# Drawing twelve attention halves into the first six parts of the weight stage, and loading the first unit's queries first

## The chip, the cores and the metric

The kernel runs on one core of one Trainium2 chip. The metric is device time in microseconds (us) of one execution, lower is better. A core has TensorE (PE), VectorE (DVE), ScalarE (ACT) and GpSimd (POOL), which run their own instruction streams in order, and SyncE (SP), whose queue issues nearly all loads of this kernel, in order as well.

## The reference, cut to what matters

Window attention over 8 heads, then two feed-forward blocks, all in float32. The last weight of the first block is only ever used behind `w3`, so the kernel may multiply `w3 @ w_out` ahead of the tokens.

```python
scores = q @ k.T / sqrt(64)            # 4 x 8 heads, 576 positions, head size 64
attn   = softmax(where(0 <= i - j < 64, scores, -1e9)) @ v
x      = attn laid out as [2304, 512]
x      = ((x @ w1) * (x @ w2)) @ w3 @ w_out      # 512 -> 1024 -> 1024 -> 512
h      = x @ w_in                                # 512 -> 2048
out    = (h * sigmoid(h)) @ w_out2               # 2048 -> 512
```

## The kernel before, in words

The weights come as 64-bit words and are converted on the chip. A chunk is 128 x 512 weights, 512 KB of words. `line` (40 chunks in the first stage) is the order in which they are worked. `loads_to(n)` issues the loads up to chunk n on SP's queue (L107). `steps_to(n)` advances the conversion: `stage0` is two ACT instructions (L114, L115), `stage1` two DVE instructions ("fraction", L125, and "sign", L128) and a POOL addition (L132). The two `stage1` pieces are put on a list, `parts`, and `fill` puts them out between other DVE instructions. Chunks of `w1` and `w2` also get a high part (ACT, L140) and a low part (DVE or POOL, L144).

The first stage, `phase_w` (L401), multiplies `w3 @ w_out`. It has 16 steps s of two parts each, 32 parts in all. A part first advances the conversion by about one chunk (`steps_to`, L468), then puts out attention (`halves_to`, L469), then four PE matmuls of 128 x 512 (L476, two accumulators, each shown as two instructions in the trace). In front of each s, `loads_to` asks for the chunks of two steps ahead (L462). By that order each engine and SP's queue meet: loads of chunks, conversion, attention, matmuls, part by part. Four accumulators are emptied after part 15 and 16 and again after part 31 and 32 (ACT and DVE, L483 by way of `split`, L79 and L82).

Attention is worked in groups g (one unit of 128 tokens, one pair of heads). A group takes two halves. Half 2g transposes the weights of group g-1 on PE (L308), makes the scores of group g (L261), and then masks and takes the row minimum on DVE (L275, two instructions), copies the transposed weights on ACT (L314) and takes the exponentials on ACT (L286). Half 2g+1 normalises on DVE (L294, L296, L298), multiplies group g-1 with its values on PE (L335 to L337), copies that on ACT (L338), and asks SP for the queries and keys of group g+2 (`load_qk`, L219 and L223, three loads) and the values of group g+2 (`load_v`, L229). The buffers of queries and keys are two, so `load_qk(g+2)` waits until PE has made the scores of group g; `load_v(g+2)` waits until PE has multiplied the values of group g-1. In the first block's groups (g < 17, "plain") this is all there is.

When enough halves are out, `split_x(0, c)` (L473) splits a quarter of the attention's output for the next stage. After the 32 parts `phase_a(0)` (L486) begins with half 28, which transposes group 13 and makes the scores of group 14. Phase A and all that follows are mostly matmuls.

Of the kernel before, what the change touches and what calls it, by code (L numbers as in the profile page):

```python
# [42 lines left out]
def tile_window_attention_ffn(ctx, tc, qkv, vp, mask, ident, w1, w2, w3t, w_out, w_in, w_out2, out):  # L43
# [15 lines left out]
    def f32(ap):  # L59
        return ap.bitcast(F32)  # L60
# [7 lines left out]
    def slot(name, tag, dims, dtype=F32, pool=None, bufs=1):  # L68

        t = (pool or main).tile([128, SLOTS.get(tag, 1024)], dtype, name=name, tag=tag, bufs=bufs)  # L70
        n = int(np.prod(dims))
        letters = "abcd"[: len(dims)]
        sizes = {x: d for x, d in zip(letters[1:], dims[1:])}
        return t[:, :n].rearrange(f"p ({' '.join(letters)}) -> p {' '.join(letters)}", **sizes)
# [14 lines left out]
    def accumulator(name, shape):  # L89

        turn[0] = (turn[0] + 1) % converting["banks"]
        return ps.tile(shape, F32, name=name, tag=f"ps{turn[0]}")
# [59 lines left out]
    def loads_to(n):  # L152
        while done["load"] < min(n, len(line)):
            if line[done["load"]]:
                line[done["load"]].load()
            done["load"] += 1
# [8 lines left out]
    def steps_to(n, lo=(nc.vector,), keep=0):  # L165

        while done["step"] < min(n, len(line)):
            t = done["step"]
            loads_to(t + 1)
            fill(len(parts))  # L170
            if t >= 1 and line[t - 1]:
                parts.extend(line[t - 1].stage1())
            fill(len(parts) - keep)
            if t >= 4 and line[t - 4]:
                line[t - 4].low_part(lo[t % len(lo)])
            if t >= 3 and line[t - 3]:
                line[t - 3].high_part()
            if line[t]:
                line[t].stage0()
            done["step"] += 1  # L180

    def drain():
        line.extend([None] * 4)
# [18 lines left out]
    def plain(g):  # L202


        return g < PLAIN

    def place(g):
        blk, r = divmod(g, 3 * NPAIR)
        return blk * 3 + r % 3, r // 3

    def load_qk(g):
        if g < NG and g not in loaded:
            loaded.add(g)
            qk_raw[g] = att.tile([128, 768], F32, name=f"qk{g}", tag="qk", bufs=2)
            u, c = place(g)
            if not plain(g):
                nc.sync.dma_start(out=qk_raw[g], in_=qkv[u, c, :, 0:768])
                return
            nc.sync.dma_start(out=qk_raw[g][:, 0:128], in_=qkv[u, c, :, 0:128])  # L219

            for h, hs in HEADS:
                n = slice(384 + h * 192, 576 + h * 192)
                nc.sync.dma_start(out=k_p[g % 2][hs, h * 192 : h * 192 + 192], in_=qkv[u, c, hs, n])  # L223

    def load_v(g):
        if g < NG and ("v", g) not in loaded:
            loaded.add(("v", g))
            if plain(g):
                nc.sync.dma_start(out=v_p[g % 3], in_=vp[g])  # L229
                return  # L230
            v_raw[g] = att.tile([128, 3, 64], F32, name=f"v{g}", tag="v", bufs=3)
            u, c = place(g)
            nc.sync.dma_start(out=v_raw[g].rearrange("p t d -> p (t d)"), in_=qkv[u, c, :, 768:960])
# [119 lines left out]
    def half(h):  # L353


        g, odd = divmod(h, 2)
        if not odd:
            t_ps = transposes(g - 1) if 1 <= g <= NG else None
            if g < NG:
                scores(g)  # L360
            if t_ps is not None:
                split_t(g - 1, t_ps)
            if g < NG:
                exps(g)
        else:
            if g < NG:
                normalise(g)
            if 1 <= g <= NG:
                values(g - 1)
            for x in (g + 1, g + 2):  # L370
                if x - g == (1 if plain(x - 2) else 2):
                    prep_qk(x)
            if g < NG:
                prep_v(g)

            for x in range(g + 2, g + 5):
                if g < (x - 2 if plain(x - 2) else x - 4):
                    break
                load_qk(x)
            for x in range(g + 1, g + 4):  # L380
                if g < (x - 2 if plain(x - 3) else x - 3):
                    break
                load_v(x)
# [3 lines left out]
    def halves_to(n):  # L387
        while halves[0] < min(n, LAST_HALF):
            half(halves[0])
            halves[0] += 1  # L390
# [8 lines left out]
    W_HALVES = 28  # L399

    def phase_w():  # L401
        wo = slot("wo", "p", [8, 512])
        q = slot("q", "q", [2304])
        for i in range(2):
            p_w.append(att.tile([128, 384], F32, name=f"pw{i}", tag="vhl", bufs=2)[:, 0:320])
        w3x = [q[:, i * 512 : i * 512 + 512] for i in range(4)]
        w3x += [att.tile([128, 512], F32, name=f"w3x{i}", tag=f"pt{i}", bufs=1) for i in range(3)]
        ring = [("st", 4)] * 4 + [(f"w{i}", 1) for i in range(20, 24)]
        words = [0]

        def add(key, src, out):
            tag, bufs = ring[words[0] % 8]
            words[0] += 1
            line.append(Chunk(key, src, (main, tag, bufs), out))

        def add_w3(s):
            sw, j = divmod(s, 8)
            add(None, w3t[j * 128 : (j + 1) * 128, sw * 512 : (sw + 1) * 512], w3x[s % 7])

        def add_w12(i):  # L420
            src = (w1, w2)[i // 8][(i % 4) * 128 : (i % 4 + 1) * 128, (i // 4 % 2) * 512 :][:, :512]
            line.append(Chunk(("12", i), src, (main, f"w{i}", 1)))

        ready, i12 = [], 0
        order = (0, 1, 2, 3, 8, 9, 10, 11, 4, 5, 6, 7, 12, 13, 14, 15)
        for s in range(16):
            if s < 8:
                add(None, w_out[s * 128 : (s + 1) * 128, :], wo[:, s])
            add_w3(s)
            ready.append(len(line) + 1)  # L430
            while i12 < W12_BY[s]:
                add_w12(order[i12])
                i12 += 1
        while i12 < 16:
            add_w12(order[i12])
            i12 += 1
        drain()
        ready += [W12_B + 24 + (4 if W12_B == 16 else 0)] * 2

        for t in k_p + [f32(t) for t in k_lo]:  # L440
            for h, hs in HEADS:
                nc.gpsimd.memset(t[hs, 192 - h * 192 : 384 - h * 192], 0.0)
        loads_to(2)
        load_qk(0)
        nc.sync.dma_start(out=mask_sb[:, 1], in_=mask[:, 1])
        loads_to(3)
        nc.sync.dma_start(out=id_sb, in_=ident)
        load_v(0)
        load_qk(1)
        loads_to(5)  # L450
        nc.sync.dma_start(out=mask_sb[:, 0], in_=mask[:, 0])
        load_v(1)
        loads_to(6)
        load_v(2)
        steps_to(ready[0])
        nc.sync.dma_start(out=mask_sb[:, 2], in_=mask[:, 2])
        half(0)
        halves[0] = 1
        acc, split_done = {}, set()
        for s in range(16):  # L460
            sw, j = divmod(s, 8)
            loads_to(ready[s + 2] + (3 if s > 1 else 0))  # L462
            if j == 0:
                for i in range(4):
                    acc[i] = accumulator(f"accw{sw}_{i}", [128, 512])
            for part in range(2):
                first = ready[s + 1 if s else 0]
                steps_to(first + (ready[s + 2] - first) * (part + 1) // 2, (nc.vector, nc.gpsimd), 3)  # L468
                halves_to(min(W_HALVES, 2 + W_HALVES * (2 * s + part + 1) // 32))  # L469
                for c in range(4):  # L470
                    if halves[0] >= 6 * c + 8 and (0, c) not in split_done:
                        split_done.add((0, c))
                        split_x(0, c)  # L473
                fill(3)
                for i in (0, 1) if part == 0 else (2, 3):
                    nc.tensor.matmul(  # L476
                        acc[i], lhsT=w3x[s % 7][:, i * 128 : (i + 1) * 128], rhs=wo[:, j],
                        start=(j == 0), stop=(j == 7),
                    )
                    if j == 7:  # L480
                        n = sw * 4 + i
                        wp[n] = slot(f"wp{n}", f"w{16 + n}", [2, 512], F32R)
                        split(wp[n][:, 0], wp[n][:, 1], acc[i], "act", "dve")  # L483
# [272 lines left out]
```

## Time and profile before

| | us |
|---|---|
| three runs | 884.69, 1725.24, 883.5 |
| their median | 884.69 |
| the profiled execution | 884.13 |
| its span, first to last instruction | 882.3 |
| first part's matmuls begin | 9.65 |
| sixth part's matmuls begin | 30.81 |
| half 28, the end of the 32 parts | 103.88 |

The span is what the trace shows; 1.8 us of the execution lie around it. The second of the three runs took twice the time of the others and stands for nothing in the kernel. Rows of the timeline are: start in us, duration in us, engine, line, operation, output<-input, count, and in brackets the idle time before it and what ended that.

### The profile page before, as it was taken

The numbers are of one execution on the slowest core, as the hardware profiler recorded it, in microseconds if no ns is written. First come the engines' busy times: TensorE is split into PE (matmuls) and PEld (weight loads), VectorE is DVE, ScalarE is ACT, GpSimd is POOL, SyncE is SP. The second block draws the span as 40 slices with busy tenths as digits, with TensorE's granted clock in tenths as the row PEclk, the third lists the DMA queues.
The fourth block names the chain that finished last, engine by engine and source line by source line (L and its number), as shares of the span: only waits on it lengthen the run. The fifth ranks groups of instructions, "written<-read, shape, count | busy, mean of one in ns | idle before, by whom it ended". The sixth has DMA issues, their size and how long they took to land.

```text
span 882.3 us, 13255 instructions
## 1 busy us (share of the span) xinstructions
PE 856.0 (97%) x4362; PEld 737.0 (84%) x4362; DVE 480.7 (54%) x1202; ACT 491.0 (56%) x1219; POOL 430.6 (49%) x474
## 2 busy tenths in 40 slices
PE   4998999999999999999999999999999999999997
PEld 2454689999999999999999888888888888888896
DVE  5889888878888888888365886111111111111111
ACT  5778677788787788787475775222222222222322
POOL 4558476466466466465395787222322232222222
PEclk9999999999999999999999999999999999999999
DMA  8888423333432323331477500200020001000100
GB/s 286 295 251 262 134 79 99 125 99 100 127 94 90 126 90 100 119 99 50 182 277 261 202 0 1 77 20 0 1 89 7 0 1 51 22 0 1 48 1 25
DMA packets 43205, 85.84 MB, mean 97 GB/s; under 512 B 4864, under 2 KB 22528, under 8 KB 43136
## 3 DMA queue, kind: packets, MB, share of 16 engines
q1 hardware_dynamic: 37088, 75.55, 26.4%
q10 hardware_dynamic: 6048, 9.44, 2.9%
q8 instruction: 35, 0.57, 0.3%
q14 instruction: 34, 0.28, 0.1%
HBM read 75.53 MB, written 9.44 MB: 96 GB/s over the span
## 4 chain that ended last, share of the span: by engine, by line
PE 86%; DVE 2%; POOL 1%; issue 1%; ACT 0%; DMA 0%; POOLq 0%; SPq 0%; DVEq 0%
PE h L627 23%; PE o L646 22%; PE ab L504 21%; PE x L524 11%; PE t L308 2%; PE o L343 2%; PE s L265 1%; PE s L269 1%; PE accw L476 1%; PE o L344 1%; POOL klo L244 1%; DVE cv_b L128 0%; DVE cv_z L125 0%; DVE rs L294 0%; PE s L261 0%
## 5 line engine op out<-in xcount | busy, mean ns | idle before, releaser
L82 POOL TENSOR_TENSOR g<-sg,g 128x512 fp32r<-128x512 f32 (+1 forms) x80 | 94.8, 1185 | 250.0 <-ACT g L79 237.3
L627 PE MATMUL h<-x2t,hl 128*128 128x512 f32 (+1 forms) x960 | 213.4, 371 | 0.0
L646 PE MATMUL o<-hl,g 128*128 128x512 f32 x864 | 211.2, 392 | 0.4 <-ACT g L79 0.3
L633 DVE TENSOR_TENSOR sg<-h,sg 128x512 f32<-128x512 f32 (+1 forms) x80 | 51.1, 638 | 288.5 <-ACT sg L632 288.5
L627 PEld LDWEIGHTS h<-x2t,hl 128*128 128x128 f32 x960 | 169.4, 188 | 33.8
L646 PEld LDWEIGHTS o<-hl,g 128*128 128x128 f32 x864 | 160.9, 188 | 35.9 <-ACT g L79 0.8
L632 ACT ACTIVATE sg<-h 128x512 f32<-128x512 f32 (+1 forms) x80 | 44.4, 555 | 195.4 <-PE h L627 195.4
L504 PE MATMUL ab<-xa,hl 128*128 128x384 f32 x576 | 117.1, 338 | 0.0
L504 PE MATMUL ab<-xb,hl 128*128 128x384 f32 x576 | 115.6, 335 | 0.0
L504 PEld LDWEIGHTS ab<-xb,hl 128*128 128x128 f32 x576 | 101.4, 188 | 0.0
L504 PEld LDWEIGHTS ab<-xa,hl 128*128 128x128 f32 x576 | 99.8, 188 | 0.8
L351 POOL TENSOR_TENSOR xr<-ot 128x128 f32<-128x128 f32 x55 | 33.2, 603 | 118.5 <-DVE ot L350 116.5
L132 POOL TENSOR_TENSOR cv_b<-cv_b,cv_r 128x512 int32<-128x512 int32 x48 | 73.6, 1534 | 26.8 <-DVE cv_b L128 11.2
L79 ACT CAST g<-sg 128x512 fp32r<-128x512 f32 (+1 forms) x80 | 46.3, 579 | 63.5 <-DVE sg L633 61.8
L286 ACT ACTIVATE sm<-sm,nm 128x192 f32<-128x192 f32 x144 | 64.4, 448 | 17.7 <-DVE nm L275 16.6
L244 POOL TENSOR_TENSOR klo<-qk,qkhi 64x192 fp32r<-64x192 f32 x110 | 70.1, 637 | 5.7 <-ACT qkhi L240 1.5
L524 PE MATMUL x<-p,wp 128*128 128x384 f32 x360 | 69.6, 335 | 0.0
L524 PEld LDWEIGHTS x<-p,wp 128*128 128x128 f32 x360 | 62.2, 188 | 0.1
L125 DVE TENSOR_SCALAR cv_z<-cv_b 128x512 int32<-128x512 int32 x72 | 49.4, 686 | 17.0 <-ACT cv_b L114 16.6
L114 ACT ACTIVATE cv_b<-words 128x512 f32<-128x512 f32 x72 | 48.2, 670 | 11.5 <-DMA words<-in_w_out 5.6
L128 DVE SCALAR_TENSOR_TENSOR cv_b<-words,cv_z 128x512 int32<-128x512 int32 x72 | 49.4, 686 | 3.5 <-issue 0.5
L275 DVE CUSTOM_DVE_ANT_0 sm<-s,mask_sb 128x192 f32<-128x192 f32 x144 | 45.7, 354 | 6.6 <-PE s L261 3.6
(82 smaller groups left out, 1258.9 us busy)
## 6 DMA issues: line engine op xcount, KB each, us to landing
qk<-in_qkv SPq DMA_DIRECT2D x55, 384.0 KB, 3.1
words<-in_w_out SPq DMA_DIRECT2D x24, 512.0 KB, 8.4
words<-in_w3t SPq DMA_DIRECT2D x16, 512.0 KB, 6.2
words<-in_w SPq DMA_DIRECT2D x16, 512.0 KB, 6.2
words<-in_w_in SPq DMA_DIRECT2D x16, 512.0 KB, 6.8
v<-in_qkv SPq DMA_DIRECT2D x55, 96.0 KB, 2.7
x2d<-x2s ACTq DMA_DIRECT2D x24, 192.0 KB, 1.9
out_x<-osb ACTq DMA_DIRECT2D x18, 256.0 KB, 2.1
```

The source lines that it names most:

```text
L82: (nc.vector if eng_lo == "dve" else nc.gpsimd).tensor_tensor(out=lo, in0=src, in1=f32(hi), op=ALU.subtract)
L114: nc.scalar.activation(out=f32(self.b), in_=f32(self.high), func=AF.Copy, scale=2.0**-112)
L125: nc.vector.tensor_scalar(out=self.z, in0=b, scalar1=3, scalar2=None, op0=ALU.logical_shift_left)
L128: nc.vector.scalar_tensor_tensor(out=b, in0=self.high, scalar=-0x80000000, in1=self.z, op0=ALU.bitwise_and, op1=ALU.bitwise_or)
L132: nc.gpsimd.tensor_tensor(out=x, in0=b, in1=self.r, op=ALU.add)
L244: nc.gpsimd.tensor_tensor(out=k_lo[g % 2][hs, h * 192 : h * 192 + 192], in0=t[hs, n], in1=f32(hi[hs, n]), op=ALU.subtract)
L286: nc.scalar.activation(out=x, in_=x, func=AF.Exp, scale=-1.0, bias=nm[:, h : h + 1], accum_out=rs[:, h : h + 1])
L504: nc.tensor.matmul(acc, lhsT=w[:, l, fs], rhs=x[k // 2][:, k % 2, r, :], start=(k == 0 and n == 0), stop=(k == 3 and n == 2),)
L524: nc.tensor.matmul(acc, lhsT=wp[f][:, l, o * 128 : (o + 1) * 128], rhs=p[f][:, r, :], start=(f == 0 and n == 0), stop=(f == 7 and n == 2),)
L627: nc.tensor.matmul(acc, lhsT=weights["in", f // 4, k][:, l, fs], rhs=x[:, k, r, :], start=(k == 0 and i == 0), stop=(k == 3 and i == 2),)
L633: nc.vector.tensor_tensor(out=sg, in0=acc, in1=sg, op=ALU.mult)
L646: nc.tensor.matmul(oacc[t], lhsT=g[:, l, t * 128 : (t + 1) * 128], rhs=weights["out", f][:, r, :], start=(f == 0 and i == 0), stop=(f == 1 ...
```

## The change

Two edits, both in `phase_w`. The loads of group 0's queries and keys are issued ahead of the first two chunks instead of behind them. The count of halves up to part n (n from 1 to 32) becomes 2 + min(2n, 9 + 17n // 32) instead of 2 + 28n // 32, both at most 28.

```diff
                 nc.gpsimd.memset(t[hs, 192 - h * 192 : 384 - h * 192], 0.0)
+        load_qk(0)
         loads_to(2)
-        load_qk(0)
         nc.sync.dma_start(out=mask_sb[:, 1], in_=mask[:, 1])
...
                 steps_to(first + (ready[s + 2] - first) * (part + 1) // 2, (nc.vector, nc.gpsimd), 3)
-                halves_to(min(W_HALVES, 2 + W_HALVES * (2 * s + part + 1) // 32))
+
+                n = 2 * s + part + 1
+                halves_to(min(W_HALVES, 2 + min(2 * n, 9 + 17 * n // 32)))
                 for c in range(4):
```

Worked out, the halves that are out and the chunks whose `stage0` is out, after each part:

| part | 1 | 2 | 3 | 4 | 5 | 6 | 7 | 8 | 16 | 24 | 30 | 31 | 32 |
|---|---|---|---|---|---|---|---|---|---|---|---|---|---|
| halves before | 2 | 3 | 4 | 5 | 6 | 7 | 8 | 9 | 16 | 23 | 28 | 28 | 28 |
| halves after | 4 | 6 | 8 | 10 | 12 | 14 | 14 | 15 | 19 | 23 | 26 | 27 | 28 |
| chunks, both | 5 | 7 | 8 | 9 | 10 | 12 | 13 | 14 | 22 | 31 | 37 | 37 | 37 |

Half 0 is out before the parts begin. Loads of chunks asked for at the start of a step s are the same in both: up to 7 at s = 0 (parts 1 and 2), 9 at s = 1 (parts 3 and 4), 15 at s = 2 (parts 5 and 6), 17 at s = 3.

## Rows read from the trace of the kernel before

**Rows 1.** The page, chain that ended last: shares of the span by engine
```profile
PE 86%; DVE 2%; POOL 1%; issue 1%; ACT 0%; DMA 0%; POOLq 0%; SPq 0%; DVEq 0%
```
**Rows 2.** Windows: stretch, length, busy PE PEld DVE ACT POOL, clock, DMA share, GB/s
```profile
0.00:20.00 20.00, 8.28 (x15) 3.02 (x15) 10.37 (x24) 10.51 (x19) 10.15 (x18) 1.00 0.87 294
20.00:32.70 12.70, 12.11 (x38) 6.47 (x38) 8.64 (x21) 8.96 (x24) 5.96 (x6) 0.87 0.85 289
32.70:60.00 27.30, 24.88 (x90) 13.47 (x91) 23.82 (x56) 20.48 (x53) 17.40 (x13) 1.00 0.83 265
60.00:104.50 44.50, 39.13 (x135) 20.22 (x134) 41.69 (x87) 34.06 (x82) 32.08 (x27) 1.00 0.74 224
```
**Rows 3.** Waits from 0 to 104 us: us in total, times, longest
```profile
DVE cv_z L125 <- ACT cv_b L114: 10.0, 7, 5.2
...
ACT cv_b L114 <- DMA words<-in_w_out: 5.6, 3, 2.4
```
**Rows 4.** Waits of SP's queue from 0 to 110 us
```profile
SPq L219 <- PE s L261: 24.1, 11, 5.8
SPq L229 <- PE o L337: 11.9, 11, 2.5
```
**Rows 5.** Timeline, the first 20 us, all engines
```profile
0.74 0.40 SPq L107 DMA_DIRECT2D words<-in_w_out  x1
...
4.46 0.66 ACT L114 ACTIVATE cv_b<-words 128x512 f32<-128x512 f32 x1 [2.44 <-DMA words<-in_w_out]
...
9.21 0.66 ACT L114 ACTIVATE cv_b<-words 128x512 f32<-128x512 f32 x1 [1.91 <-DMA words<-in_w_out]
...
10.33 0.44 ACT L286 ACTIVATE sm<-sm,nm 128x192 f32<-128x192 f32 x1
...
12.90 0.66 ACT L114 ACTIVATE cv_b<-words 128x512 f32<-128x512 f32 x1 [1.60 <-DMA words<-in_w3t]
...
15.12 0.56 DVE L298 TENSOR_TENSOR sm<-sm,rs 128x384 f32<-128x384 f32 x1
...
16.13 0.81 PE L261 MATMUL s<-kp,qk 128*128 128x384 f32 x2
```
**Rows 6.** Timeline, DVE: group 14's softmax, with no conversion put between
```profile
105.30 0.35 DVE L275 CUSTOM_DVE_ANT_0 sm<-s,mask_sb 128x192 f32<-128x192 f32 x1
...
106.77 0.17 DVE L294 TENSOR_SCALAR rs<-rs 128x2 f32<-128x2 f32 x1 [0.83 <-ACT sm L286]
...
107.17 0.56 DVE L298 TENSOR_TENSOR sm<-sm,rs 128x384 f32<-128x384 f32 x1
```
**Rows 7.** Groups of DVE's instructions from 32.7 to 104.5 us
```profile
L125 DVE TENSOR_SCALAR cv_z<-cv_b 128x512 int32<-128x512 int32 x25 | 17.2, 686 | 0.4
L128 DVE SCALAR_TENSOR_TENSOR cv_b<-words,cv_z 128x512 int32<-128x512 int32 x25 | 17.1, 685 | 1.5 <-issue 0.5
L275 DVE CUSTOM_DVE_ANT_0 sm<-s,mask_sb 128x192 f32<-128x192 f32 x22 | 6.9, 353 | 1.4 <-PE s L261 1.4
...
L294 DVE TENSOR_SCALAR rs<-rs 128x2 f32<-128x2 f32 x11 | 5.6, 510 | 0.7 <-ACT sm L286 0.7
L82 DVE TENSOR_TENSOR wp<-accw,wp 128x512 fp32r<-128x512 f32 x7 | 4.6, 687 | 1.9 <-ACT wp L79 1.9
```
**Rows 8.** Timeline, SP: the first of chunks 9 to 14
```profile
22.29 0.37 SPq L107 DMA_DIRECT2D words<-in_w_out  x1
```
**Rows 9.** The page, DMA issues: count, KB each, median us to landing
```profile
words<-in_w3t SPq DMA_DIRECT2D x16, 512.0 KB, 6.2
```
**Rows 10.** Timeline, PE: part 6's matmuls, those of parts 30 to 32, half 28
```profile
30.81 1.88 PE L476 MATMUL accw<-wo,q 128*128 128x512 f32 x4
...
98.67 5.37 PE L476 MATMUL accw<-wo,q 128*128 128x512 f32 x12
...
103.88 0.49 PE L308 MATMUL t<-id_sb,sm 128*128 128x128 f32 x3
```
**Rows 11.** Timeline, DVE: group 3's second minimum; group 13's normalising
```profile
32.72 0.35 DVE L275 CUSTOM_DVE_ANT_0 sm<-s,mask_sb 128x192 f32<-128x192 f32 x1
...
101.19 0.56 DVE L298 TENSOR_TENSOR sm<-sm,rs 128x384 f32<-128x384 f32 x1
```

## The prediction

> **What bounds the kernel now.** I read the chain first: 86% of it is PE [rows 1], so over the whole span matmuls set the time, and a change of order can pay only where PE stands idle. The windows show where that is: PE is busy 8.28 of the first 20 us, 12.11 of the next 12.7, and about nine tenths from there to 104.5 us [rows 2]. So the first stage is the place, and half 28, at 103.88 us [rows 10], is where its loss or gain is handed on. Inside the stage two stretches differ. Up to 32.7 us DVE works 10.37 + 8.64 = 19.0 us and has some 13.7 us free [rows 2]; what it waits for is ACT's first conversion instruction (10.0 us), and that for words on the DMA [rows 3], while the DMA is 0.85 to 0.87 busy [rows 2]. The start is bound by the arrival of chunks. From 32.7 on DVE is busy 23.82 of 27.3 and 41.69 of 44.5 us [rows 2]: there DVE is the bound. The change moves attention from the second stretch into the first, which reads well. What it does to the order of SP's queue reads badly: SP already stood 24.1 us waiting for scores before it could load queries, and 11.9 us for values [rows 4], and the loads of chunks stand behind those waits.
>
> **The queries first.** Three loads go ahead of two chunks, so chunks 0 and 1 come some 1.2 us later (three issues, by the 0.40 us of the one of chunk 0 [rows 5]) and group 0's scores earlier. Neither is worth anything: the exponentials of group 0 stand on ACT behind the conversion of chunk 2, which starts on arrival at 9.21 and lets them go at 10.33; its normalising stands on DVE behind chunks 2 and 3, the latter arriving for 12.90, and ends at 15.12 + 0.56 [rows 5]. The bytes ahead of chunks 2 and 3 are the same in both orders. Bounds: -1.1 us, if the first exponentials could run ahead of chunk 2 (10.33 - 9.21), and +1.2, if the delay of chunks 0 and 1 reached the first matmuls; but these now stand behind half 3. I take 0. Group 1's scores therefore start at 16.13 as before [rows 5]: what stood ahead of them on PE was not the matmuls of part 1.
>
> **Parts 1 to 6.** Before, seven halves were out when part 6's matmuls began at 30.81 [rows 10]. Now fourteen must be, so six full groups follow each other, each waiting for the last: transposing g needs its normalising, and the scores of g+1 stand behind that on PE. From the first minimum to the end of normalising takes 107.73 - 105.30 = 2.4 us with nothing put between [rows 6]. Between normalising and the next minimum `fill` puts out a chunk's two DVE instructions, 0.686 + 0.685 = 1.4 us [rows 7], which hides the transposes and scores; that is one chunk for a group or two, seven in all from the fourth to the tenth. Group 1's minimum starts at 16.13 + 0.81 = 17.0. Sum: 17.0 + 2.4 for group 1, five more times 2.4 is 12.0, seven chunks 9.8: 41.2 us. To this come waits for chunks. SP reaches chunks 7 and 8 only behind the loads for groups 3 and 4, the last of which waits for the values of group 1, by the same steps at about 22.0; the load of chunk 7 is issued at about 22.5. Chunk 0 took from 0.74 to 4.46, 3.7 us [rows 5], so it is there at 26.2, its conversion is 1.3 us of ACT, and the exponentials of group 3 behind it are late by about 1.4. Chunks 9 to 14, issued from 22.29 before [rows 8], stand behind the values of group 6, which wait for PE's values of group 3, about 32.0: issue at 32.5, there at 36.2, and the exponentials of group 5 are late by about 1.0. With these 2.4 group 6 is normalised at 43.6 us. What the wait costs is the largest unknown: nothing, if ACT is late itself, and 2 x (6.2 - 3.7) = 5.0 more if these loads take the median of 6.2 us [rows 9]. I take 2.4, since the DMA has little else to carry at these moments and chunk 0's is the nearest row.
>
> The Trainium skill (DMA: Bandwidth & Descriptors, Anatomy of one DMA) puts a transfer at 2.0 us plus its bytes over 436 GB/s, a fit for loads issued from GpSimd; for 512 KB that is an estimate of 3.2 us. The trace's 3.7 differs by half a microsecond, and by the page's figure the two waits would be 1.4 instead of 2.4 and the sum below 1.0 shorter.
>
> **Parts 7 to 32.** At 33.0 us before (end of group 3's minimum, 32.72 + 0.35 [rows 11], with ten chunks behind it) DVE stood where it now stands at 43.6 but for attention: it still had 68.7 us to the end of group 13's normalising at 101.75 [rows 11]. Of this, three groups' minima and four groups' normalisings have been done early. A minimum is two instructions of 0.353 that overlap to about 0.57, 1.7 for three; a normalising is 0.9 us in group 14 [rows 6], and more where its first instruction lasts 0.510 on average instead of 0.17 [rows 6, 7]: 1.1 each, 4.4 (ends: 0.9 and 1.3). The 1.4 us that DVE waited for scores [rows 7] I count as gone, since halves are now rare. Against it, two of the last four accumulators must now be emptied before group 13 is normalised, as half 27 stands behind part 31: 2 x 0.687 [rows 7] less overlap and a wait for ACT, 2.0 us in all. The quarter of the output that is split early moves from one sum to the other and cancels. So 68.7 - 1.7 - 4.4 - 1.4 + 2.0 = 63.2, and group 13 is normalised at 43.6 + 63.2 = 106.8.
>
> The first normalising instruction on its 128 x 2 values lasts 0.17 alone and 0.510 on average where POOL is busy [rows 6, 7]. The Trainium skill (SBUF — State Buffer, Who interferes with whom) says that DVE and POOL share a pair of ports under an exclusive lock, and that the one that issues second waits for the whole of the other's instruction. That speaks for the change: normalisings drawn into the start, where POOL adds less, escape the lock. By the rule the four are worth 0.9 + 0.34 each where I took 1.1, and the sum would be 0.6 shorter.
>
> **The end of the stage.** Before, group 13 was ready at 101.75 but PE still had twelve matmuls to do from 98.67, so half 28 came at 103.88 [rows 10, 11]. Now attention lasts until part 32, PE has done its matmuls by then, and half 28 starts with group 13, at 106.8. This 2.1 us of cover is lost; it is what the shorter DVE list would otherwise have given. PE's own work leaves room: 26 parts of 1.8 us (5.37 for three [rows 10]) from 43.6 are done by 90, and seven groups of at most 2 us by 104. From half 28 on both orders are the same and PE is the bound, so all of 106.8 - 103.9 = 2.9 us reaches the end: 884.13 + 2.9 = 887.0. The profiled execution lies 0.56 below the median of the runs shown, which is inside what they scatter; the forecast is 887.0.
>
> **Rivals.** First, **the gap at the start is filled for nothing**, and the kernel is a little faster. For it: 13.7 us of free DVE time up to 32.7 [rows 2]. It needs no wait on chunks 7 and 9 (-2.4), and DVE without idle time in the later parts and the waits for accumulators hidden (-2.0): half 28 at 102.4, the time 882.6; with the first normalising instruction always at 0.17 some 0.6 less. Against it: SP's order is fixed by the program, and the chain of six groups leaves DVE waiting for exponentials, 0.83 us a group and more [rows 6]. Second, on the other side, **chunks are late for good**: while SP stands before the loads for groups 4 to 6 the DMA is nearly idle from about 19 to 33 us, and if the later conversion then waits for chunks instead of DVE, the loss is not made up. Its price is the 5.0 us above, with a further 1.4 for the wait on scores that stays: half 28 at 113.2, the time 893.4. It decides from part 3 on, at the load of chunk 7, and shows as ACT waiting for words after 45 us. Against it: 25 chunks in 63 us is one in 2.5 us, and before the change they came at that rate with the DMA 0.74 to 0.83 busy [rows 2] and with attention's loads beside them. Third, **a lasting starvation** in which the prefetch never recovers and the stage's end moves by 18 us or more; the windows leave the DMA too much room for that.
>
> **How the numbers follow.** The forecast, 885 to 890, has 0.52; the first rival, 879 to 885, 0.22; the second, 890 to 898, 0.23; the third 0.03. Half of the outer rivals' ranges is wanted to leave out no more than 2 in 10: 881 to 893.5. Two per cent, about what a measurement of this kernel can tell from no change, is 17.7 us, which only the third rival reaches on the slow side; on the fast side the free time of the start is itself only 13.7 us. So within 2% has 0.96, slower 0.03, faster 0.01.
>
> **What would show it.** Right: group 1's scores near 16.1; the loads of chunks 7 and of 9 to 14 near 22.5 and 32.5, the latter against 22.29; part 6's matmuls near 42 to 44 instead of 30.81; DMA share well under 0.8 between 20 and 33 us; group 13's normalising and half 28 together near 107; the rest of the trace shifted whole. Wrong: part 6 at 40 or earlier (the chain is shorter than I added up, or SP is not held), or ACT waiting for words after part 7 (the second rival), or a shift in phase A that differs from that of half 28.

## The result and the profile after

The changed kernel takes 895.75 us (median of 5 runs), the kernel before 883.86 beside it: a ratio of 1.0138, 95% interval 1.0119 to 1.0158. The ratio comes from the fast runs alone, without the one of 1725.24 us, and is not the quotient of the two medians. It is 11.9 us slower, where 3 were forecast. The profiled execution took 895.62 us with a span of 893.8, 11.5 more than before.

The windows of the changed kernel, the same stretches as before in [rows 2], and below them three of 5 us (columns as there):

```profile
0.00:20.00 20.00, 5.03 (x14) 3.09 (x15) 7.31 (x19) 9.48 (x20) 7.68 (x16) 1.00 0.78 257
20.00:32.70 12.70, 8.63 (x32) 4.71 (x31) 8.27 (x25) 7.19 (x23) 3.82 (x4) 0.88 0.48 144
32.70:60.00 27.30, 22.92 (x70) 12.09 (x69) 15.85 (x43) 14.41 (x39) 10.66 (x9) 0.81 0.66 211
60.00:104.50 44.50, 42.83 (x137) 21.24 (x137) 39.40 (x79) 36.12 (x81) 35.01 (x27) 1.00 0.90 303
...
30.00:35.00 5.00, 4.63 (x10) 2.69 (x11) 2.55 (x6) 2.60 (x9) 1.93 (x2) 0.50 0.17 47
45.00:50.00 5.00, 5.00 (x12) 2.83 (x13) 3.57 (x7) 3.80 (x10) 1.46 (x2) 0.50 1.01 391
```

Three things are to be seen. DVE, whose free time at the start was to be filled, worked 15.6 us up to 32.7 instead of 19.0 [rows 2], and 15.85 instead of 23.82 in the next stretch: early attention took the place of conversion and did not come on top of it. The DMA, 0.85 busy from 20 to 32.7 before, fell to 0.48 and then made up from 60 us on. And PE, whose clock had been 0.87 in one stretch of [rows 2] and 1.00 in the others, had a granted clock of 0.50, which is 1.2 GHz of its 2.4, in two stretches of 5 us.

How this comes about stands in four short pieces of the timeline. SP's queue, where the loads for groups 4 and 6 hold up chunks 7 and 9. It is the queries (L219) that wait, for PE's scores of groups 2 and 4, which end at 22.48 and 36.97; the keys and values follow without a further wait:

```profile
22.51 0.33 SPq L219 DMA_DIRECT2D qk<-in_qkv  x1
...
24.05 0.58 SPq L229 DMA_DIRECT2D vp<-in_vp  x1
24.68 0.43 SPq L107 DMA_DIRECT2D words<-in_w3t  x1
...
36.99 0.33 SPq L219 DMA_DIRECT2D qk<-in_qkv  x1
...
38.59 0.53 SPq L229 DMA_DIRECT2D vp<-in_vp  x1
39.23 0.36 SPq L107 DMA_DIRECT2D words<-in_w_out  x1
```

ACT, which waits for the two chunks, with the copy of a group's transposed weights (L314) behind the conversion:

```profile
28.80 0.66 ACT L114 ACTIVATE cv_b<-words 128x512 f32<-128x512 f32 x1 [3.28 <-DMA words<-in_w3t]
...
29.91 0.41 ACT L314 COPY pw<-t 128x320 f32<-128x320 f32 x1
...
43.32 0.66 ACT L114 ACTIVATE cv_b<-words 128x512 f32<-128x512 f32 x1 [4.72 <-DMA words<-in_w_out]
```

PE, which waits for that copy, and then does values, the part's matmuls, transposes and scores at half its clock; the same steps at 37.41 and 39.95 are at full clock:

```profile
30.37 0.80 PE L335 MATMUL o<-pw,vp 128*128 128x128 f32 x2 [2.69 <-ACT pw L314]
...
31.71 3.73 PE L478 MATMUL accw<-wo,q 128*128 128x512 f32 x4
35.23 0.85 PE L308 MATMUL t<-id_sb,sm 128*128 128x128 f32 x3
35.87 1.10 PE L261 MATMUL s<-kp,qk 128*128 128x384 f32 x2
...
37.41 1.94 PE L478 MATMUL accw<-wo,q 128*128 128x512 f32 x4
...
39.95 0.81 PE L261 MATMUL s<-kp,qk 128*128 128x384 f32 x2
...
44.90 0.79 PE L335 MATMUL o<-pw,vp 128*128 128x128 f32 x2 [4.14 <-ACT pw L314]
...
46.23 3.73 PE L478 MATMUL accw<-wo,q 128*128 128x512 f32 x4
```

DVE's normalising of groups 3, 4, 6 and 13, and half 28 on PE, which answers to [rows 10]:

```profile
31.64 0.56 DVE L298 TENSOR_TENSOR sm<-sm,rs 128x384 f32<-128x384 f32 x1
...
38.88 0.56 DVE L298 TENSOR_TENSOR sm<-sm,rs 128x384 f32<-128x384 f32 x1
...
52.98 0.56 DVE L298 TENSOR_TENSOR sm<-sm,rs 128x384 f32<-128x384 f32 x1
...
115.51 0.56 DVE L298 TENSOR_TENSOR sm<-sm,rs 128x384 f32<-128x384 f32 x1
```
```profile
116.22 0.52 PE L308 MATMUL t<-id_sb,sm 128*128 128x128 f32 x3 [1.95 <-DVE sm L298]
```

Half 28 comes 12.3 us later than the 103.88 of before; 0.8 of it is given back behind it. Part 6's matmuls begin at 51.70, where 42 to 44 was to show that the forecast is right. Group 6 is normalised at 53.5, against a forecast of 43.6. The whole error is made by then: from there to group 13 it takes 116.1 - 53.5 = 62.5 us, against 63.2 forecast.

### The profile page after: what moved, and what is told of

The parts are those of the page before. It is cut to its first block, busy times and chain, and to the rows that moved or that the text cites. A ratio compares the mean times of both kernels' runs of the same rounds, so it can differ in the third digit from the quotient of the medians.

```text
span 893.8 us, 13260 instructions
## 1 busy us (share of the span) xinstructions
PE 859.9 (96%) x4362; PEld 739.4 (83%) x4362; DVE 477.5 (53%) x1202; ACT 491.7 (55%) x1219; POOL 428.3 (48%) x474
## 4 chain that ended last, share of the span: by engine, by line
PE 83%; DVE 3%; issue 1%; POOL 1%; ACT 0%; POOLq 0%; DVEq 0%
PE h L629 22%; PE o L648 22%; PE ab L506 21%; PE x L526 11%; PE t L308 2%; PE o L343 2%; PE s L265 1%; PE s L269 1%; PE o L344 1%; DVE cv_b L128 1%; DVE cv_z L125 1%; DVE hl L144 1%; POOL klo L244 0%; DVE rs L294 0%; POOL p L82 0%
## 5 line engine op out<-in xcount | busy, mean ns | idle before, releaser
L308 PEld LDWEIGHTS t<-id_sb,sm 128*128 128x128 f32 x216 | 27.9, 145 | 31.1 <-ACT cv_r L115 16.6
L308 PE MATMUL t<-id_sb,sm 128*128 128x128 f32 x216 | 36.5, 279 | 17.6 <-DVE sm L298 16.4
```

The costliest lines, as they stand in the source:

```text
L308: nc.tensor.transpose(t_ps[:, i * 128 : i * 128 + 128], x[:, at : at + 128], id_sb)
```

## The experiments

Theories: **late chunks** (loads of chunks stand on SP's queue behind loads that wait for attention, and all else follows from it), **cold PE** (the half clock after each idle stretch is a loss of its own), **chain** (six groups behind one another are too long, whatever the loads do), and **lost cover** (the last halves now stand in parts 31 and 32). Each ratio is against runs of the kernel before on the same chip.

**The loads of chunks ahead.** Before `halves_to` in the changed kernel:

```diff
+                if n == 1:
+                    halves_to(2)
+                if n <= 6:
+                    loads_to((9, 11, 13, 15, 16, 17)[n - 1])
                 halves_to(min(W_HALVES, 2 + min(2 * n, 9 + 17 * n // 32)))
```

> The changed kernel, with the loads of chunks 7 to 16 issued two by two ahead of the attention of parts 1 to 6 instead of behind that of parts 2, 4 and 6. Late-chunks theory: ACT no longer waits 3.3 us for chunk 7 and 4.7 us for chunk 9, PE does not stand idle behind it and stays at its full clock, group 6 is normalised near 45 us instead of 53.5, the time is near 887. Chain theory (six groups behind one another are too long in themselves, whatever the chunks do): group 6 at 50 or later, the time 892 or more.

886.44 us, ratio 1.0036 (1.0024 to 1.0047). Three quarters of the loss are gone. Its trace on SP (chunks 7 and 9), ACT's waits for words up to 60 us, and group 6 on DVE:

```profile
16.23 0.58 SPq L107 DMA_DIRECT2D words<-in_w3t  x1
...
21.09 0.36 SPq L107 DMA_DIRECT2D words<-in_w_out  x1
```
```profile
ACT cv_b L114 <- DMA words<-in_w_out: 5.5, 2, 4.8
...
ACT cv_b L114 <- DMA words<-in_w3t: 1.7, 2, 1.5
```
```profile
42.78 0.56 DVE L298 TENSOR_TENSOR sm<-sm,rs 128x384 f32<-128x384 f32 x1
```

The waits that are left are those of the first 20 us, 4.8 of them for chunk 0. Group 6 is normalised at 43.3, and PE's granted clock is 1.00 from 20 to 44 us with nothing done for it. Late chunks it is, and the chain theory falls.

**Only two chunks ahead.** The changed kernel with `halves_to(2)` and `loads_to(9)` in part 1 and nothing else:

> The changed kernel with only the loads of chunks 7 and 8 put ahead (behind half 1); chunks 9 to 14 stay behind the values of group 6. It sizes the two waits one by one. If the first wait and what follows from it cost 4 us, as the trace of the changed kernel has it (group 4 normalised at 39.4 instead of the 34.3 of e1_chunks_ahead), and the second 5: ACT waits for chunk 9 only, group 4 at 34 to 35, group 6 at 47 to 49, the time 890 to 892. If one wait is as bad as two, because the DMA then carries six chunks at once all the same: 894 or more.

891.37 us, ratio 1.0088 (1.0073 to 1.0103), all inside what was expected: group 4 is normalised at 35.1, and group 6 at 47.8:

```profile
47.23 0.56 DVE L298 TENSOR_TENSOR sm<-sm,rs 128x384 f32<-128x384 f32 x1
```

So each of the two waits carries about half of the time lost: 0.5%, 4.4 to 4.9 us. The split is rough, since group 1 was 0.9 us late in this run: from group 1 to group 6 it is 32.4 us in the changed kernel, 25.7 here and 22.1 with all loads ahead.

**PE kept busy.** Matmuls of no use ahead of `values`, written into the accumulator that the real ones then overwrite:

```diff
             v, p, o = v_p[g % 3], p_st.pop(g), o_ps[:, 0, 0]
+            for _ in range({2: 3, 4: 4}.get(g, 0)):
+                nc.tensor.matmul(o_ps.rearrange("p a b n -> p (a b n)"), lhsT=id_sb,
+                                 rhs=mask_sb[:, 0:2, :].rearrange("p a n -> p (a n)"), start=True, stop=True)
```

The first attempt had 3 and 5 of them, and nine more of 128 x 384 ahead of group 0's transposes:

> The changed kernel with matmuls of no use put where PE stood idle: nine ahead of group 0's transposes, three ahead of group 2's values, five ahead of group 4's; their results are overwritten. Cold-PE theory (a good part of the loss is that PE runs at half clock after each idle stretch): the granted clock is 1.0 from 30 to 35 and 45 to 50 us instead of 0.50, the work from values to scores takes 3.5 us there instead of 6.6 and 6.2, the time falls by 4 to 7 us to 889 to 892. Late-chunks theory alone (what PE does while it waits does not matter): 894 to 896.

895.52 us, ratio 1.0137 (1.0118 to 1.0156). The nine outlasted their gap and made group 0's transposes 3 us late and the end of group 1 2.0 us, so the time says little. Behind group 1 the trace says more. Its windows, and the normalising of groups 3 and 4:

```profile
30.00:35.00 5.00, 4.90 (x18) 2.35 (x17) 2.08 (x9) 3.84 (x10) 1.64 (x2) 1.00 0.47 155
45.00:50.00 5.00, 3.63 (x15) 2.01 (x16) 3.13 (x7) 4.86 (x13) 1.00 (x1) 1.00 0.95 361
```
```profile
33.58 0.56 DVE L298 TENSOR_TENSOR sm<-sm,rs 128x384 f32<-128x384 f32 x1
...
37.86 0.56 DVE L298 TENSOR_TENSOR sm<-sm,rs 128x384 f32<-128x384 f32 x1
```

At full clock group 4 takes 4.3 us, with chunk 7 as late as before, where the changed kernel takes 7.2. From the end of group 1 to that of group 6 it is 29.7 us, against 32.4 in the changed kernel and 22.1 with the loads ahead. The second attempt left the nine out:

> The changed kernel with matmuls of no use in two gaps only, three ahead of group 2's values and four ahead of group 4's (in e2_pe_filled the nine ahead of group 0's transposes outlasted their gap and made these 3 us late). Cold-PE theory: from values to scores 3.5 us in both places instead of 6.6 and 6.2, group 6 normalised 2 to 5 us earlier than in the changed kernel (53.5), the time 890 to 893. Late-chunks theory alone: 894 to 896.

894.11 us, ratio 1.0121 (1.0108 to 1.0134), which the changed kernel's interval overlaps. Its windows, PE behind the two filled gaps, and group 6:

```profile
30.00:35.00 5.00, 3.83 (x17) 2.01 (x15) 2.31 (x6) 4.08 (x11) 1.00 (x1) 1.00 0.35 113
45.00:50.00 5.00, 3.16 (x15) 1.80 (x14) 3.64 (x11) 4.74 (x12) 2.55 (x2) 0.94 0.93 344
49.00:54.50 5.50, 5.50 (x14) 2.43 (x13) 4.44 (x9) 2.77 (x7) 3.19 (x4) 0.69 0.68 179
```
```profile
48.42 0.49 PE L337 MATMUL o<-pw,vp 128*128 128x128 f32 x2 [1.84 <-ACT pw L314]
...
49.14 5.35 PE L480 MATMUL accw<-wo,q 128*128 128x512 f32 x8
```
```profile
49.69 0.56 DVE L298 TENSOR_TENSOR sm<-sm,rs 128x384 f32<-128x384 f32 x1
```

In the two filled gaps the clock stays up, group 4 takes 4.3 us again, and group 6 is normalised at 50.3, 3.3 us earlier than in the changed kernel. But half 28 comes at 115.35, only 0.9 earlier, and the time does not follow. PE now waits 1.84 us for the copy of group 5's weights, which stands on ACT behind chunks 10 and 11, and behind that wait its clock falls instead: 0.69 on average from 49 to 54.5 us, and eight matmuls of parts 6 and 7 take 5.35 us where the changed kernel took 3.65. Part 8's matmuls begin at 55.30, 0.9 us earlier than in the changed kernel (56.16), and from there to half 28 it is 60.1 us in both. So what is lost again of the 3.3 us is lost before part 8.

The half clock follows the waits: with the chunks in time it does not come up, and with two gaps filled it moved to a third. It isn't the cause of the 12 us, but it carries a part of them. Of the 10.3 us that late chunks cost between groups 1 and 6 (32.4 against 22.1) it is 2.7 by the first attempt and 3.5 by the second (28.8 us), an estimate from one profiled execution each.

**One edit at a time.** The kernel before with the first edit alone, and the changed kernel without it:

> The kernel before with the first edit alone (group 0's queries and keys ahead of two chunks). The prediction's step: no gain, since group 0's exponentials stand behind chunk 2; within 1.2 us of the kernel before. If the first edit is what delays group 1's scores by the 1.1 us seen in the changed kernel, 884 to 886; if it gains anything, below 883.

> The changed kernel without the first edit (the order of the first loads as before, the halves early). If the halves carry the loss: 894 to 896, the changed kernel's less the 1.1 us of the first edit or a little more. If the first edit carries it: near 884.

The queries alone: 884.7 us, ratio 1.0014 (1.0004 to 1.0024). The halves alone: 893.89 us, ratio 1.0123 (1.0101 to 1.0145). The halves carry the loss. The queries cost about a tenth of a per cent, and the windows of the first 5 us show a likely reason, first before, then with the queries first:

```profile
0.00:5.00 5.00, 0.00 (x0) 0.00 (x0) 0.00 (x0) 1.82 (x2) 2.22 (x12) 1.00 0.64 221
```
```profile
0.00:5.00 5.00, 0.84 (x2) 0.50 (x2) 0.00 (x0) 1.28 (x1) 2.22 (x12) 1.00 0.41 101
```

With the three small loads first, the DMA moves 101 GB/s in these 5 us instead of 221, while SP is busy issuing; 0.6 MB are missing, about one chunk, in the stretch that waits for chunks. That the tenth is lost there is argued, not shown: in the trace of the queries alone half 28 comes at 103.39, 0.5 us before that of the kernel before.

**The end.** What was left of the loss in the first experiment was looked for at the end of the stage, where PE waits for groups 12 and 13 (the kernel with chunks ahead):

```profile
98.34 0.52 PE L308 MATMUL t<-id_sb,sm 128*128 128x128 f32 x3 [1.44 <-DVE sm L298]
...
105.57 0.52 PE L308 MATMUL t<-id_sb,sm 128*128 128x128 f32 x3 [1.96 <-DVE sm L298]
```

In that kernel the divisor 32 was made 30, so that 28 halves are out after part 30:

```diff
-                halves_to(min(W_HALVES, 2 + min(2 * n, 9 + 17 * n // 32)))
+                halves_to(min(W_HALVES, 2 + min(2 * n, 9 + 17 * n // 30)))
```

> e1_chunks_ahead with the halves reaching 28 at part 30 as in the kernel before (17n // 30 in place of 17n // 32), so that the matmuls of parts 30 to 32 again lie behind the last normalising. Lost-cover theory (what is left of e1's loss is made at the end, where halves 26 and 27 stand in parts 31 and 32): half 28 at 102 to 103.5 us instead of 105.6, PE idle for less than 1 us ahead of the last two transposes instead of 3.4, the time 882 to 884. Rival (DVE's list is the bound, and its order does not matter): half 28 at 105 or later, 886 to 887.

882.77 us, ratio 0.9998 (0.9989 to 1.0006): 0.4% less than without, and level with the kernel before. In the program the twelve matmuls stand behind the last normalising again:

```profile
94.53 0.52 PE L308 MATMUL t<-id_sb,sm 128*128 128x128 f32 x3 [0.69 <-DVE sm L298]
...
98.39 5.37 PE L482 MATMUL accw<-wo,q 128*128 128x512 f32 x12
...
103.59 0.49 PE L308 MATMUL t<-id_sb,sm 128*128 128x128 f32 x3
```

Half 28 comes 2.0 us earlier (103.59 against 105.57). The rest of the 0.4% arises behind it. In the profiled execution of the kernel with chunks ahead, PE's clock fell after the wait of 1.96 us:

```profile
106.00:110.00 4.00, 4.00 (x14) 3.49 (x14) 2.51 (x10) 1.41 (x5) 0.00 (x0) 0.57 0.16 41
```

From half 28 to the next transposes it is 7.44 us there and 5.82 with the end covered. In the changed kernel, where PE waited 1.95 us at the same place, it is 5.84, at full clock.

The same with the first loads in their old order:

> e5_end_cover without the first edit (first loads in the order of before). If the first edit costs about 1 us at the start of the chain, 0.5 to 2 us below e5_end_cover; if it is worth nothing, the same within 0.5 us.

881.38 us, ratio 0.9985 (0.9977 to 0.9994), half 28 at 102.08: 1.5 us earlier than with the queries first, and the time 1.4 lower.

**Is the burst worth anything?** A control, the loads ahead in the kernel before with its own halves:

> The kernel before with the loads of chunks issued ahead as in e1_chunks_ahead, its halves and first loads as they were. A control: how much of e1's time is due to the loads alone. If early loads help the old order as well: 880 to 882. If the old order did not lack chunks after the first 20 us: 883 to 885, and e1's loss against it is the price of early halves as such.

882.02 us, ratio 0.9989 (0.9981 to 0.9998). The loads alone gain a tenth of a per cent in the old order, and the burst of six parts (0.9985, with the end covered) adds nothing to it that can be told. A shorter burst, of four parts, in the kernel with end cover and old loads:

```diff
-                halves_to(min(W_HALVES, 2 + min(2 * n, 9 + 17 * n // 30)))
+                halves_to(min(W_HALVES, 2 + min(2 * n, 6 + 20 * n // 30)))
```

> e8_end_cover_old_loads with a shorter burst: 2 + min(2n, 6 + 20n // 30) halves, so that attention runs ahead for four parts instead of six. If DVE's free time at the start is there to be filled, a shorter burst fills less of it: 882 to 883.5, above e8. If the burst is worth nothing in itself and the loads ahead are what gains, it is the same as e8 and e6_before_chunks_ahead within 0.1%: 881 to 882.

880.9 us, ratio 0.9973 (0.9962 to 0.9983): below both of the two expectations, though its interval overlaps that of the burst of six. It was run again beside the control on one chip:

> e6_before_chunks_ahead again, on one chip with e12: does a burst of attention gain anything once the loads are ahead? If the loads alone carry the gain: this and e12 the same within 0.1% of the kernel before, both near 881 to 882.

> e10_burst_of_four again, beside e11. If the burst of four parts gains by itself: 0.1 to 0.3% below e11, the intervals apart.

The control 882.25 us, ratio 0.9988 (0.9978 to 0.9997); the burst of four 880.67 us, ratio 0.9963 (0.9951 to 0.9975), the intervals apart. It beats both kernels, the one before by 2.8 us. The windows of the control and then of the burst:

```profile
0.00:20.00 20.00, 9.73 (x14) 4.06 (x15) 10.76 (x24) 11.00 (x21) 10.22 (x18) 1.00 0.88 289
20.00:32.70 12.70, 11.40 (x40) 6.29 (x39) 9.27 (x25) 10.09 (x27) 7.14 (x5) 1.00 1.00 341
32.70:60.00 27.30, 26.49 (x96) 14.12 (x94) 23.77 (x56) 20.76 (x53) 16.40 (x13) 1.00 0.83 260
```
```profile
0.00:20.00 20.00, 5.78 (x15) 3.52 (x16) 7.96 (x22) 10.21 (x22) 7.67 (x16) 1.00 0.88 288
20.00:32.70 12.70, 12.00 (x48) 6.32 (x47) 9.68 (x30) 8.89 (x27) 6.08 (x5) 1.00 0.93 318
32.70:60.00 27.30, 25.30 (x88) 13.34 (x87) 25.85 (x55) 20.50 (x50) 17.33 (x13) 1.00 0.83 266
```

Even here DVE works less up to 32.7 us than in the control (17.6 against 20.0): the free time at the start is not filled by any of these orders. The burst has DVE busier later, 25.85 of 27.3 us against 23.77, and by 60 us both have done about the same, 43.5 and 43.8 us. Half 28 comes at 101.52 instead of 102.14; the other 0.9 of the 1.5 us between the two spans arises behind it, as 0.8 did in the changed kernel, and was not followed. Whether four parts do better than six, and why, isn't shown by these runs.

## Why the prediction was wrong, step by step

**The queries first, taken as 0: nearly right.** The sign was open and turned out as a small loss, by 0.14% alone, which is the 1.2 us of the upper bound. The step said that the bytes ahead of chunks 2 and 3 are the same in both orders. They are, but the bytes come later: the three loads took SP 1.7 us instead of the 1.2 reckoned (chunk 0 is issued at 2.43 instead of 0.74 [rows 5]), with the DMA half idle meanwhile, and ACT begins with chunk 2 at 10.35 instead of 9.21 [rows 5]. Group 1's scores start at 17.26 instead of 16.13.

**Parts 1 to 6, 43.6 against 53.5: the step that failed.** Its chain was sound: with the chunks there in time group 6 is normalised at 43.3, though group 1 is 1.8 us late. The forecast also had SP's queue held by attention, and the two waits at chunks 7 and 9. What failed is the term "with these 2.4". I priced a late chunk by how much later the exponentials behind it start, and took PE's work as hidden behind DVE's. But the copy of the group's transposed weights stands behind that chunk on ACT too; PE's values wait for the copy, the part's matmuls stand behind the values, and the next group's transposes and scores behind the matmuls, most of it at 1.2 GHz after PE's idle time. So the delay reaches the next group: group 4 took 39.4 - 32.2 = 7.2 us where 3.8 were reckoned and no chunk was late. With PE kept busy in the gap it took 4.3, so about 3.0 of these 3.4 us are the half clock, which my sum had nowhere, and 0.5 the order on PE. And since the scores of group 4 (and not, as the prediction has it, the values of group 3) are what SP last waits for before it goes on to chunk 9, the second wait began from a queue already late, issued at 39.23 instead of the reckoned 32.5. Against the sum, group 1 was 1.8 late, groups 2 and 3 together 0.6, group 4 3.4, group 5 2.5, group 6 1.6: 9.9 us. By the runs, each of the two waits, with the half clock that follows it, is worth 4.4 to 4.9 us of the end, against the 1.4 and 1.0 of the sum. Even the upper bound, 2.4 + 5.0 = 7.4 for both, lies below the 9.3 us that they came to (895.75 against 886.44).

**A transfer's duration, taken as 3.7:** 28.80 - 24.68 = 4.1 and 43.32 - 39.23 = 4.1. The DMA did have something else to carry: it was 0.83 and 0.79 busy in these stretches, with the chunks that are issued right behind. The Trainium skill (DMA: Bandwidth & Descriptors, Anatomy of one DMA) gives 3.2 as an estimate for loads issued from GpSimd; these loads, from SP, took 0.9 more. The size of this error is 0.4 us a wait, and it did not decide.

**Parts 7 to 32, 63.2 against 62.5: right, in part by luck.** DVE is nearly without waits there, as reckoned (4.2 of the 62.5 us), though PE is nearly as full (busy for 57.7). The normalisings are 4.9 us less than before (4.4 reckoned), and the wait for scores is gone. But the two accumulators cost some 4.2 us (1.4 of work and 2.8 of waiting for ACT), where 2.0 were reckoned, and DVE's casts and low parts (L81, L144) 3.7 less, where nothing was. The two errors have opposite signs.

**The end, right:** half 28 follows group 13 by 0.15 us, and the end-cover experiment puts the cover at 2.0 us of half 28, near the 2.1 forecast.

**The rivals.** The second, chunks late for good, gave 893.4, the nearest in time, and it named the right place, the load of chunk 7. Its mark, ACT waiting for words after 45 us, is missing: 0.2 us from 45 to 104. The lateness ended, but what it had cost wasn't made up. The first rival, the gap filled for nothing, falls: even with the loads ahead DVE works 17.2 to 18.0 us up to 32.7 in the early orders, less than the 19.0 of before. No rival had PE's clock in it. The range ended at 893.5, inside the second rival's, which was itself priced with the same too short chain of waiters.

## What to carry to other kernels

A load that waits for a buffer holds up every load behind it on its queue, as SP's rows show here. Before work is drawn forward, put the loads that nothing holds up ahead of those that it brings along: here that turned a loss of 1.4% into one of 0.4%, and with the end of the stage covered again and the first loads in their old order into a gain of 0.15%, of which the loads ahead bring 0.11% in the old order too. To price a late arrival, follow the waiting engine's queue to everything behind it, through each engine in turn, until the chain comes back to the load that is next, and ask what PE's clock will be when it starts again: here the half clock made most of what a wait cost the group after it. And free time of one engine need not be there to be filled: in none of the early orders did DVE do more by 32.7 us than before.

## What the runs showed that was not expected

After PE had stood idle 2.69 and 4.14 us its work ran at 1.2 GHz from 30 to 35 and 45 to 50 us: four matmuls in 3.73 us instead of 1.94. With matmuls of no use in the gap it did not, and yet the kernel was hardly faster, since the clock fell behind the next gap instead, 0.50 from 50 to 52 us after 1.84 idle. An idle time of 1.96 us at half 28 was followed by such a fall in the kernel with chunks ahead, and one of 1.95 in the changed kernel was not.

DVE's cast for the early split of the output, in the changed kernel up to 60 us and after:

```profile
L81 DVE CAST xa<-xr 128x384 fp32r<-128x384 f32 x2 | 0.7, 357 | 0.1
```
```profile
L81 DVE CAST xb<-xr 128x384 fp32r<-128x384 f32 x1 | 1.4, 1423 | 0.0
```

The same cast takes 0.36 us where POOL stands idle, as it did then, and 1.42 later among POOL's additions. The Trainium skill (SBUF — State Buffer, Who interferes with whom) says that a DVE cast can take the pair of ports that DVE and POOL share, and that whichever of the two issues second waits for the whole instruction of the other. The trace agrees, with a price of 1.07 us for this cast: it starts at 80.15, during a POOL addition (79.71 to 81.36), and ends 0.2 us after that. It is a gain of early attention that the prediction took to cancel out, and too small to be seen in the time.
